# A new written order for all engines of a strided convolution with its gradients

## The chip, the cores and the metric

The kernel runs on one core of a Trainium2 chip. The time is that of one execution on the device, in microseconds (us). A core has several engines with queues of their own: TensorE (PE; its weight loads are listed as PEld), VectorE (DVE), ScalarE (ACT), GpSimd (POOL) and SyncE (SP), which here issues DMA transfers only. Each engine takes its instructions strictly in the order in which they were written; between engines semaphores make an instruction wait for those on whose results it depends.

## What is computed

The forward pass is a convolution over time with stride 2, a normalisation of each channel over all positions, and a tanh-GELU. The kernel returns its output and the gradients by all four inputs for a given output gradient.

```python
B, T, D, K = 2, 16000, 256, 31          # x [2,16000,256], w [31,256,256], bf16

def _fwd_reference(x, w, gn_gamma, gn_beta):
    L = (T - K) // 2 + 1                # 7985
    h = sum of einsum('blc,cd->bld', x[:, i:i + 2 * L:2, :], w[i]) over i < K
    mu = einsum('bld->bd', h)[:, None, :] / L
    var = einsum('bld->bd', (h - mu) ** 2)[:, None, :] / L
    h = (h - mu) / sqrt(var + 1e-5) * gn_gamma + gn_beta
    return gelu(h, approximate=True)

def reference(x, w, gn_gamma, gn_beta, grad_out):
    out, vjp = jax.vjp(_fwd_reference, x, w, gn_gamma, gn_beta)
    return (out, *vjp(grad_out))        # out, dx, dw, dgamma, dbeta
```

## The kernel before

**Stages.** The work is written in five stages, each with its own use of one large SBUF buffer (`arena`; nearly all tiles are pieces of it and bear its name in the profile) and of four PSUM pairs (`ps`).

- F0: convolution of batch 0, in four chunks (`forward`, L709). Three nested levels of a fast algorithm for short filters replace products by sums: DVE forms sums of the input (`tt` of `f_sums`, L509) and of the weights (`w_sub`, L493), PE multiplies (`f_mm`, L551), ACT copies PSUM tiles (`keep`, L646) and DVE adds them as starting values ("seeds", `ve`, L631).
- F1: convolution of batch 1, beside it the statistics and the GELU with its derivative for batch 0 (`gelu_unit`, L901: ACT at L911, L913, L918, L920 and L937, DVE at L916, L922, L926 and L939).
- G0: the input gradient of the first chunks (`input_grad`, L1360; PE at L1235, ACT copies at L1268, seeds at L1312, sums of the results at L1338, sums of planes at L1133), beside it the GELU of batch 1. Four steps prepare the gradient of the convolution's output: `e_load`, `e_comp` (L1096, L1098, L1100 on DVE, L1103 on ACT).
- G1: the rest of the input gradient (`g_planes`, L1183, `g_piece`, L1322). In G0 and G1 `dl_turn` (L1110) transposes what the weight gradient needs: SP issues a transpose (`turn`, L352), POOL stores the result to DRAM (`load`, L347, to tiles `dld`).
- W: the weight gradient in nine rounds n = 0 to 8 (`weight_grad`, L1637). Each round loads gradient tiles (`d_tile`, L1503, from `dld`) and x tiles (`x_raw`, L1468, from DRAM), forms sums (L1466, L1579, L1583, L1594, L1599, L1679, L1684), multiplies (L1513), seeds (`w_both`, L1623) and writes (`w_emit`, L1542). In some rounds `out0_late` (L959) transposes and stores the second batch's output.

**What sets the order.** Helpers such as `add` (L223) do not issue an instruction. `Plan` collects 3469 operations, each with its engine, the function that issues its instructions, and the earlier operations on which it depends (`preds`), worked out from the memory that it reads and writes. The number of an operation is the count of the call of `add` that made it: F0 has 0 to 699, F1 700 to 1250, G0 1251 to 1951, G1 1952 to 2872, W 2873 to 3468. At the end `emit` goes through the constant tuple `SEQUENCE` (L39), which lists every number once, and issues the operations in that order:

```python
assert all(place[p] < place[i] for i, o in enumerate(self.ops) for p in o["preds"])
for i in SEQUENCE:
    r = self.ops[i]["fn"]()
    ...
    pin(r)
```

So an engine's queue is the part of `SEQUENCE` that holds its numbers; DMA issues of SP and POOL are in such queues too. An operation of PE is a group of matmuls, 8 of them in most of G0.

**Operations named below.**

| number | engine, line | what it does |
|---|---|---|
| 259 | SP L347 | writes zeros to a `dld` tile |
| 22 to 29 | SP L347 | loads of weights |
| 1235, 1232 | DVE L631, L509 | last seed of F1, and a sum |
| 1349 | SP L347 | stores a GELU output tile to `yd` |
| 1352, 1354 | ACT L911 | first GELU step of the next tile; overwrites the tile that 1349 reads |
| 1353, 1355 | ACT L913 | second GELU step; DVE 1356 (L916) needs them |
| 1345, 1347 | ACT L937 | copies with a sum; 1346, 1348 (DVE L939) are their partners |
| 1602, 1608 | ACT L646 | keeps of PSUM tiles |
| 1599 | ACT L1268 | copy of a PSUM tile; needs PE 1598 |
| 1603, 1604 | PE L1235 | need 1599 |
| 1609, 1611 | PE L1235 | 1609 needs 1602, 1611 needs 1608; 1608 needs 1603 and 1604 |
| 1606 | PE L1235 | between them |
| 1558, 1620 | DVE L1338, L1133 | sum of a result, sum of planes |
| 1796 | DVE L1061 | scales a plane loaded by 1791 (SP) |
| 1924 | ACT L1268 | copy of a PSUM tile; 1486 and 1897 are ACT too |
| 1951 | DVE L1183 | difference of planes |
| 2839, 2840 | SP L352 | transposes of `dl_turn` |
| 2841, 2842, 2845, 2846 | POOL L347 | stores of their and other results to `dld` |
| 2886, 2885 | SP L347 | `d_tile` loads of round 0 |
| 2944, 2945, 2943 | SP L347 | `x_raw` loads for round 1; 2944 uses memory that the stores read, 2945 waits for PE 2916, 2943 for DVE 2911 |
| 2877 | SP L352 | transpose of `out0_late` |
| 2948, 2949, 2947 | SP L347 | `d_tile` loads of round 1 |
| 2960, 2964 | PE L1513, DVE L1599 | first product and a difference of round 1 |
| 3436 | DVE L631 | seed near the end of W |

Of the kernel before, what the change touches and what calls it, by code (L numbers as in the profile page):

```python
# [34 lines left out]
def mmt(n):  # L35
# [4 lines left out]
    4, 11, 5, 6, 12, 7, 8, 10, 1, 3, 14, 2, 13, 21, 15, 16, 30, 31, 37, 39, 34, 32, 33, 36,  # L40
    40, 35, 19, 38, 41, 42, 46, 43, 49, 17, 45, 51, 44, 48, 52, 53, 50, 18, 54, 55, 47, 60, 20, 66,
    259, 65, 22, 61, 24, 84, 67, 25, 85, 23, 83, 86, 26, 87, 77, 28, 62, 29, 27, 79, 88, 171, 63, 59,
    71, 91, 68, 58, 89, 64, 57, 69, 93, 56, 70, 72, 94, 238, 170, 74, 90, 95, 73, 172, 96, 97, 105, 99,
    98, 101, 75, 107, 106, 111, 100, 92, 112, 102, 108, 76, 109, 113, 110, 130, 123, 122, 131, 114, 104, 196, 124, 137,
    125, 133, 78, 132, 115, 134, 103, 135, 267, 116, 136, 239, 144, 154, 186, 117, 173, 120, 146, 80, 118, 119, 155, 199,
    127, 145, 148, 156, 126, 157, 128, 147, 197, 129, 158, 151, 152, 159, 121, 149, 150, 160, 176, 138, 167, 139, 182, 140,
    177, 198, 174, 141, 142, 168, 161, 162, 153, 143, 201, 163, 169, 166, 207, 202, 183, 203, 175, 206, 178, 251, 200, 187,
    227, 209, 184, 205, 229, 185, 226, 180, 223, 81, 188, 189, 208, 9, 277, 247, 164, 228, 179, 181, 225, 210, 263, 165,
    255, 214, 283, 243, 213, 211, 0, 289, 204, 290, 231, 230, 82, 222, 292, 192, 190, 224, 212, 193, 279, 191, 278, 234,
    215, 312, 280, 232, 291, 313, 281, 216, 282, 235, 293, 381, 218, 220, 299, 194, 217, 219, 300, 236, 301, 302, 237, 297,  # L50
    303, 379, 221, 295, 304, 294, 233, 326, 285, 284, 314, 287, 319, 286, 353, 306, 288, 298, 305, 354, 296, 328, 307, 308,
    195, 327, 352, 309, 315, 378, 329, 310, 316, 317, 330, 318, 311, 337, 333, 336, 356, 332, 334, 340, 355, 331, 341, 349,
    380, 339, 320, 338, 321, 350, 322, 358, 357, 342, 351, 324, 369, 343, 359, 344, 382, 365, 323, 364, 368, 387, 383, 325,
    245, 250, 346, 348, 395, 345, 360, 408, 384, 362, 361, 385, 396, 252, 386, 366, 241, 394, 405, 370, 276, 404, 335, 253,
    264, 397, 242, 420, 371, 388, 271, 406, 367, 249, 390, 240, 246, 426, 363, 389, 258, 392, 432, 257, 409, 268, 254, 455,
    410, 261, 411, 256, 412, 372, 244, 391, 347, 407, 375, 414, 275, 422, 421, 248, 373, 393, 270, 403, 413, 398, 374, 423,
    416, 456, 433, 424, 425, 400, 442, 401, 417, 532, 533, 399, 443, 402, 444, 418, 445, 419, 446, 262, 274, 376, 427, 272,
    269, 447, 457, 497, 428, 462, 531, 448, 435, 434, 430, 265, 260, 449, 377, 495, 429, 450, 436, 529, 441, 431, 458, 439,
    469, 438, 437, 471, 440, 273, 459, 452, 470, 460, 496, 461, 415, 479, 472, 498, 453, 480, 530, 454, 473, 481, 451, 475,
    463, 476, 477, 499, 464, 474, 501, 500, 492, 482, 266, 465, 502, 507, 483, 511, 467, 503, 508, 484, 493, 512, 504, 485,  # L60
    539, 486, 487, 494, 466, 491, 535, 468, 489, 509, 560, 505, 488, 478, 548, 513, 536, 514, 537, 547, 490, 534, 541, 572,
    538, 540, 562, 542, 546, 556, 544, 557, 564, 515, 558, 543, 584, 518, 559, 506, 545, 516, 561, 566, 510, 573, 574, 555,
# [4 lines left out]
    527, 621, 690, 673, 652, 653, 675, 623, 676, 691, 644, 646, 686, 650, 677, 924, 685, 654, 688, 692, 678, 528, 687, 651,  # L67
    945, 679, 699, 680, 938, 645, 693, 931, 695, 925, 664, 667, 946, 711, 944, 681, 930, 932, 683, 689, 694, 655, 969, 657,
    682, 933, 951, 926, 684, 659, 700, 940, 927, 696, 668, 658, 697, 663, 656, 970, 928, 701, 929, 702, 935, 934, 937, 936,
    939, 942, 698, 971, 661, 665, 703, 704, 705, 947, 941, 706, 943, 952, 712, 666, 948, 660, 707, 708, 662, 709, 710, 960,  # L70
    736, 972, 916, 961, 954, 716, 949, 714, 713, 953, 715, 963, 717, 950, 739, 957, 965, 974, 1016, 955, 996, 718, 959, 956,
    962, 737, 973, 975, 720, 976, 977, 721, 719, 731, 958, 964, 984, 967, 732, 966, 983, 722, 986, 979, 723, 724, 733, 734,
    725, 980, 981, 968, 726, 729, 735, 728, 727, 1017, 988, 738, 730, 740, 987, 760, 982, 741, 998, 990, 985, 999, 978, 742,
    989, 997, 1043, 1000, 744, 1001, 743, 745, 1006, 1002, 995, 1007, 746, 991, 1008, 1041, 992, 747, 1004, 763, 748, 761, 749, 1009,
    754, 755, 751, 1003, 1018, 753, 756, 752, 762, 759, 764, 1012, 993, 765, 1010, 750, 766, 1011, 757, 768, 758, 784, 1023, 1005,
    1044, 769, 767, 1019, 1014, 1013, 770, 1024, 771, 785, 994, 1042, 772, 787, 1015, 1025, 773, 1032, 777, 783, 776, 1020, 775, 1033,
    778, 786, 1089, 1021, 1022, 788, 1088, 780, 1029, 1027, 789, 1028, 779, 1026, 1031, 808, 1030, 1068, 790, 1034, 782, 1035, 1039, 781,
    791, 792, 1051, 793, 1037, 794, 804, 809, 1050, 803, 1046, 1053, 795, 774, 796, 1070, 1047, 1036, 1040, 1048, 1038, 1052, 805, 797,
    811, 1069, 807, 799, 800, 1061, 801, 1045, 810, 802, 812, 1059, 832, 1049, 1056, 1054, 806, 813, 1055, 1071, 1114, 1117, 1072, 1073,
    1079, 1058, 1074, 814, 1078, 1113, 816, 1057, 1080, 815, 817, 1060, 1090, 1115, 835, 818, 1067, 819, 833, 1081, 798, 820, 1063, 1075,  # L80
    1116, 821, 824, 823, 1082, 825, 1076, 828, 826, 834, 836, 858, 831, 1062, 1084, 837, 1077, 1158, 838, 1091, 827, 1095, 839, 1083,
    840, 841, 861, 842, 830, 1092, 1093, 829, 1094, 1064, 843, 1066, 1100, 1101, 1086, 1065, 1102, 844, 859, 851, 1103, 1085, 1104, 1096,
    822, 852, 845, 1111, 847, 855, 856, 848, 849, 1130, 850, 860, 1124, 1098, 885, 862, 853, 1087, 1097, 846, 854, 863, 857, 1118,
    864, 1105, 1119, 865, 1112, 866, 1125, 888, 867, 886, 868, 878, 1106, 1099, 869, 1107, 877, 1126, 870, 1132, 1127, 1109, 871, 1131,
    1134, 873, 883, 876, 882, 887, 884, 1129, 1145, 875, 879, 874, 1160, 1128, 889, 1164, 1277, 880, 1108, 1144, 881, 890, 1133, 1147,
    872, 1110, 1146, 1148, 1155, 891, 1263, 1159, 893, 892, 894, 1149, 1150, 904, 895, 896, 905, 897, 1135, 1151, 1170, 1136, 1161, 1162,
    1152, 898, 1137, 1181, 907, 1120, 900, 906, 1138, 908, 901, 1163, 1172, 1154, 902, 899, 903, 1171, 1139, 1180, 1121, 1142, 1275, 1278,
    1279, 1183, 1141, 1280, 1140, 1143, 1174, 1156, 1182, 1267, 909, 1194, 1166, 1290, 1165, 1157, 1173, 1122, 1167, 1177, 1176, 1185, 1193, 1175,
    1168, 1123, 1282, 1184, 1169, 1265, 910, 1187, 1200, 1291, 1178, 1186, 911, 1208, 1196, 1188, 1264, 1195, 1281, 1209, 1190, 1197, 1153, 1210,
    1211, 1198, 1205, 1199, 1179, 1212, 1218, 912, 1191, 1219, 913, 920, 1216, 914, 1202, 1192, 1215, 1201, 917, 1189, 1213, 1221, 1214, 1204,  # L90
    918, 919, 1233, 1203, 1222, 1206, 1269, 1220, 921, 1217, 1223, 1271, 922, 1224, 923, 1234, 1226, 1292, 1237, 1227, 1293, 1230, 1225, 1283,
    1236, 1284, 1268, 1239, 1294, 1238, 1285, 1295, 1321, 1296, 1232, 1286, 1235, 1297, 1298, 1287, 1320, 1266, 1243, 1276, 1288, 1289, 1242, 1207,
    1270, 1309, 1311, 1307, 1330, 1245, 1228, 1308, 1310, 1518, 1312, 1229, 1300, 1240, 1247, 1299, 1520, 1241, 1519, 1244, 1533, 1521, 1522, 1301,
    1526, 1272, 1246, 1322, 1231, 1527, 1323, 1250, 1528, 1303, 1532, 1324, 1304, 1248, 1302, 1545, 1650, 1314, 1273, 1325, 1305, 1306, 1540, 1313,
    1249, 1315, 1539, 1251, 1534, 1316, 1641, 1252, 1538, 1326, 1523, 1253, 1567, 1254, 1317, 1255, 1256, 1535, 1327, 1328, 1524, 1257, 1318, 1544,
    1258, 1649, 1636, 915, 1329, 1274, 1529, 1525, 1259, 1260, 1261, 1262, 1673, 1319, 1334, 1536, 1651, 1541, 1530, 1333, 1640, 1658, 1537, 1562,
    1332, 1549, 1674, 1566, 1542, 1331, 1507, 1652, 1543, 1550, 1563, 1335, 1546, 1531, 1351, 1548, 1570, 1568, 1555, 1653, 1336, 1556, 1571, 1564,
# [1750 lines left out]
```

## Time and profile before

| | us |
|---|---|
| three runs | 1136.36, 1140.59, 1136.03 |
| their median | 1136.36 |
| the profiled execution | 1133.3 |
| its span | 1131.5 |

The span goes from the first to the last instruction of the profiled execution; 1.8 us of that execution's own time lie outside it. The mean granted TensorE clock was 0.995 of full speed.

In the profile a row of the timeline gives the start and the length of a group of like instructions on one engine, the engine, the line, the operation, the tile written and the tile read, the shape, the count, and in square brackets the idle time of the engine ahead of it with the engine and tile that ended this idle time. SPq is the queue of SP: there the length is the time that the queue was taken by the issue. A row of the windows gives, for a stretch, the busy time of each engine with its count, the granted TensorE clock, the busy share of the DMA engines and the rate in GB/s. A row of the waits gives for an engine and line what it waited for: the total, the number of times, the longest.

### The profile page before, as it was taken

The page shows a single profiled execution, that of the slowest core. Times are in us where ns is not written, and L with a number is a line of the kernel's source. Part 1 is how long each engine was busy: PE and PEld are TensorE (multiplying, and loading weights), DVE is VectorE, ACT ScalarE, POOL GpSimd, SP SyncE. Part 2 cuts the span into 40 slices and gives each one's busy share as a digit, 9 for nine tenths or more (in the row PEclk, how much of TensorE's full clock was granted, in tenths as well). Part 3 has the DMA queues.
Part 4 walks back from the last instruction along what each step waited for, and adds up shares of the span by engine and source line. Part 5 has one row for each costly group of instructions (what it writes and reads, how often), then busy time and mean ns, then how long its engine had stood idle before and what let it go on. Part 6 is the DMA issues. An engine that isn't in the chain of part 4 may idle for free. (4 is left out here: it accounts for less than half of the span.)

```text
span 1131.5 us, 19151 instructions
## 1 busy us (share of the span) xinstructions
PE 1097.4 (97%) x7642; PEld 751.2 (66%) x7688; DVE 1029.5 (91%) x1031; ACT 557.3 (49%) x826; POOL 135.9 (12%) x212
## 2 busy tenths in 40 slices
PE   6999999999999989899999999999999999999997
PEld 4888899877777874344444444444488886666786
DVE  7998798769999999899999989889999999889997
ACT  1244444378788669677867666564312212111200
POOL 0000000000000022332222233333110000000000
PEclk9999999999999999899999999999999999999999
DMA  9678868969897799999986687899999707999655
GB/s 233 117 218 207 221 203 231 215 136 204 194 191 211 227 322 288 264 252 266 255 215 183 163 207 204 202 214 220 258 310 230 269 10 256 355 327 299 212 160 159
DMA packets 360407, 251.97 MB, mean 223 GB/s; under 512 B 234487, under 2 KB 327933, under 8 KB 358141
## 3 DMA queue, kind: packets, MB, share of 16 engines
q1 hardware_dynamic: 353213, 231.86, 76.3%
q0 software_dynamic: 7104, 18.89, 6.2%
q8 instruction: 60, 0.98, 0.4%
q14 instruction: 30, 0.25, 0.1%
HBM read 110.43 MB, written 84.45 MB: 172 GB/s over the span
## 5 line engine op out<-in xcount | busy, mean ns | idle before, releaser
L551 PE MATMUL ps<-arena 128*128 128x256 bf16 (+4 forms) x3460 | 407.3, 281 | 12.4 <-DMA arena<-in_x_dram 5.5
L1235 PE MATMUL ps<-arena 128*128 128x512 bf16 x1775 | 390.9, 378 | 9.7 <-ACT ps L1268 4.5
L551 PEld LDWEIGHTS <-arena 128*128 128x128 bf16 x3460 | 337.2, 98 | 82.2 <-issue 6.6
L1235 PEld LDWEIGHTS <-arena 128*128 128x128 bf16 x1812 | 178.1, 98 | 220.8 <-issue 16.8
L1513 PE MATMUL ps<-arena 128*128 128x256 bf16 (+1 forms) x2407 | 300.1, 286 | 5.2 <-DVE ps L1623 1.4
L1513 PEld LDWEIGHTS <-arena 128*128 128x128 bf16 x2416 | 235.9, 98 | 70.1 <-issue 5.4
L646 ACT ACTIVATE arena<-ps 128x1024 f32<-128x1024 f32 x126 | 126.2, 1022 | 255.2 <-PE ps L1513 103.4
L509 DVE TENSOR_TENSOR arena<-arena 128x2080 bf16<-128x2080 bf16 (+7 forms) x125 | 154.8, 1265 | 15.1 <-PE ps L551 14.4
L347 POOL DMA_DIRECT2D dld<-arena x144 | 104.5, 728 | 253.5 <-DMA arena<-arena 228.8
L926 DVE TENSOR_TENSOR arena<-arena 128x2048 bf16<-128x2048 bf16 (+1 forms) x80 | 95.4, 1197 | 3.6 <-ACT arena L918 1.0
L1466 DVE TENSOR_TENSOR arena<-arena 128x4096 bf16<-128x4096 bf16 (+1 forms) x50 | 87.9, 1775 | 7.1 <-DMA arena<-in_x_dram 6.2
L1312 DVE TENSOR_TENSOR ps<-ps,arena 128x1024 f32<-128x1024 f32 x60 | 72.5, 1227 | 6.6 <-PE ps L1235 3.5
L1183 DVE TENSOR_TENSOR arena<-arena 128x1032 bf16<-128x1032 bf16 (+1 forms) x110 | 72.4, 691 | 4.5 <-PE ps L1235 2.4
L666 ACT ACTIVATE arena<-ps 128x512 bf16<-128x512 f32 (+1 forms) x64 | 37.0, 580 | 53.2 <-PE ps L551 49.3
L356 POOL MEMSET arena<- 128x128 bf16 (+9 forms) x31 | 8.2, 286 | 400.5 <-DVE arena L509 239.4
L1615 ACT COPY ps<-ps 128x256 f32<-128x256 f32 x54 | 19.2, 359 | 70.5 <-PE ps L1513 69.3
L1322 DVE TENSOR_TENSOR arena<-ps,arena 128x1024 bf16<-128x1024 f32 x40 | 48.3, 1219 | 4.4 <-PE ps L1235 4.2
L1599 DVE TENSOR_TENSOR arena<-arena 128x2048 bf16<-128x2048 bf16 x42 | 50.5, 1221 | 0.0
L916 DVE SCALAR_TENSOR_TENSOR arena<-arena 128x2048 bf16<-128x2048 bf16 (+1 forms) x16 | 35.8, 2239 | 14.1 <-ACT arena L913 7.4
L587 ACT ACTIVATE ps<-ps 128x256 f32<-128x256 f32 x72 | 26.7, 370 | 39.8 <-PE ps L551 38.7
L1583 DVE TENSOR_TENSOR arena<-arena 128x2048 bf16<-128x2048 bf16 x38 | 45.5, 1220 | 0.1
L911 ACT ACTIVATE arena<-arena,stats 128x1024 bf16<-128x1024 bf16 (+1 forms) x32 | 37.9, 1212 | 8.8 <-DMA yd<-arena 8.8
(89 smaller groups left out, 794.9 us busy)
## 6 DMA issues: line engine op xcount, KB each, us to landing
arena<-in_x_dram SPq DMA_DIRECT2D x24, 1024.0 KB
dld<-arena POOLq DMA_DIRECT2D x144, 128.0 KB, 4.0
arena<-in_x_dram SPq DMA_DIRECT2D x34, 512.0 KB
out_dram<-arena SPq DMA_DIRECT2D x31, 512.0 KB
arena<-hd SPq DMA_DIRECT2D x24, 512.0 KB
arena<-dld SPq DMA_DIRECT2D x18, 640.0 KB
arena<-dld SPq DMA_DIRECT2D x18, 576.0 KB
vl<-arena SPq DMA_DIRECT2D x36, 256.0 KB
```

Of the source, the lines that this page charges most:

```text
L347: lambda: e.dma_start(out=out, in_=in_), dma=np_ * ns / 16e3 * 1.03, ns=ns, tp=SH[pk], slack=slack)
L509: lambda: nc.vector.tensor_tensor(out=o, in0=a, in1=b, op=ALU.add))
L551: yield nc.tensor.matmul(ps[:, dh, cs], lhsT=wt, rhs=mv, start=s0, stop=False, skip_group_check=True)
L646: lambda: nc.scalar.activation(out=out, in_=ps, func=ACT.Copy, scale=scale))
L926: add("DVE", dve(nf), [o], [a, b_], lambda: V.tensor_tensor(out=o, in0=a, in1=b_, op=op))
L1183: lambda: nc.vector.tensor_tensor(out=o, in0=a, in1=b, op=ALU.subtract))
L1235: yield nc.tensor.matmul(ps[:, e, 0:wide], lhsT=lt, rhs=mv, start=s0, stop=False, skip_group_check=True)
L1312: lambda ps=ps, g=g: nc.vector.tensor_tensor(out=ps[:], in0=px[:], in1=g, op=ALU.add))
L1322: lambda: nc.vector.tensor_tensor(out=ho[:, :, k, :], in0=ps[:], in1=g, op=ALU.add))
L1466: add("DVE", dve(o.free_size()), [o], [a, b], lambda: nc.vector.tensor_tensor(out=o, in0=a, in1=b, op=ALU.add))
L1513: yield nc.tensor.matmul(ps[:, s, c0:c1], lhsT=lt, rhs=mv, start=s0, stop=False, skip_group_check=True)
L1599: add("DVE", dve(2048), [o], [u, v], lambda o=o, u=u, v=v: nc.vector.tensor_tensor(out=o, in0=u, in1=v, op=ALU.subtract))
```

## The change

Only the tuple `SEQUENCE` is different. It holds the same 3469 numbers, so the same instructions on the same tiles are issued, and every operation still comes behind those on which it depends. The change describes itself as planned anew on twelve draws of varying transfer times and means of two profiles.

Instructions whose place in the queue of their engine is another one: 169 of 931 on PE (by up to 5 places), 280 of 999 on DVE (up to 11), 152 of 689 on ACT (up to 12), 95 of 208 on POOL (up to 7), 282 of 642 on SP (up to 9). They lie in many short blocks over the whole kernel, within which the numbers are rearranged; between the blocks the queues agree.

All 136 lines that are replaced are lists of such numbers. Below are those that hold the operations of the table.

```diff
@@ -37,151 +37,151 @@
-    259, 65, 22, 61, 24, 84, 67, 25, 85, 23, 83, 86, 26, 87, 77, 28, 62, 29, 27, 79, 88, 171, 63, 59,
...
-    1654, 1578, 1646, 1341, 1575, 1647, 1600, 1655, 1553, 1648, 1352, 1781, 1579, 1557, 1342, 1354, 1343, 1576, 1602, 1598, 1577, 1346, 1605, 1344,
-    1345, 1780, 1583, 1558, 1599, 1347, 1603, 1620, 1350, 1609, 1353, 1348, 1604, 1355, 1796, 1606, 1608, 1356, 1610, 1611, 1560, 1582, 1623, 1357,
...
-    1236, 1284, 1268, 1239, 1294, 1238, 1285, 1295, 1321, 1296, 1232, 1286, 1235, 1297, 1298, 1287, 1320, 1266, 1243, 1276, 1288, 1289, 1242, 1207,
...
-    1923, 1926, 1897, 1904, 1489, 1982, 1924, 1909, 1951, 1941, 2042, 1912, 1952, 1487, 1930, 1908, 1981, 1933, 1490, 1986, 1491, 2044, 1928, 1985,
...
-    2856, 2834, 2850, 2888, 2862, 2857, 2886, 2851, 2858, 2839, 2863, 2893, 2885, 2883, 2859, 2866, 2864, 2861, 2894, 2946, 2841, 2865, 2907, 2845,
-    2899, 2846, 2908, 2895, 2842, 2900, 2903, 2901, 2868, 2904, 2896, 2902, 2897, 2869, 2906, 2898, 2905, 2913, 2912, 2867, 2915, 2944, 2870, 2860,
-    2950, 2914, 2891, 2872, 2871, 2892, 2916, 2911, 2910, 2919, 2945, 2923, 2943, 2917, 2909, 2924, 2920, 2928, 2936, 2947, 2948, 2930, 2935, 2877,
-    2929, 2931, 2937, 2921, 2940, 2980, 2918, 2932, 2922, 2952, 2933, 2938, 2951, 2949, 2941, 2880, 2939, 2954, 2934, 2925, 2953, 2942, 2966, 2960,
...
-    3435, 3440, 3451, 3379, 3436, 3386, 3390, 3437, 3447, 3397, 3456, 3452, 3448, 3444, 3458, 3453, 3445, 3402, 3449, 3457, 3398, 3446, 3400, 3459,
...
+    24, 65, 22, 61, 84, 83, 25, 85, 23, 67, 86, 28, 87, 77, 259, 29, 62, 26, 27, 79, 88, 59, 63, 89,
...
+    1292, 1225, 1284, 1238, 1294, 1268, 1239, 1240, 1285, 1321, 1295, 1296, 1232, 1297, 1286, 1235, 1298, 1287, 1320, 1270, 1243, 1276, 1308, 1288,
...
+    1340, 1646, 1781, 1578, 1654, 1341, 1601, 1647, 1655, 1579, 1553, 1648, 1352, 1342, 1598, 1602, 1557, 1576, 1343, 1354, 1577, 1620, 1599, 1344,
+    1605, 1345, 1796, 1780, 1558, 1583, 1347, 1348, 1609, 1582, 1353, 1604, 1346, 1603, 1560, 1355, 1350, 1606, 1608, 1356, 1610, 1611, 1623, 1357,
...
+    1475, 2009, 1913, 1478, 1484, 1906, 1910, 1482, 1903, 1896, 1483, 1883, 1914, 1882, 1485, 1899, 1878, 1923, 1900, 1895, 1925, 1924, 1950, 1486,
...
+    1945, 1951, 2002, 1943, 1953, 1998, 1952, 1946, 2001, 1944, 1996, 1947, 1995, 1500, 1911, 2004, 1997, 2003, 1501, 2012, 2000, 1502, 2013, 2037,
...
+    2839, 2855, 2834, 2850, 2829, 2886, 2888, 2862, 2857, 2885, 2851, 2858, 2946, 2863, 2842, 2859, 2846, 2866, 2841, 2907, 2894, 2845, 2893, 2908,
+    2865, 2864, 2895, 2904, 2899, 2903, 2896, 2868, 2906, 2944, 2900, 2897, 2912, 2901, 2869, 2902, 2898, 2913, 2867, 2905, 2915, 2870, 2891, 2872,
+    2914, 2950, 2871, 2892, 2860, 2916, 2861, 2911, 2923, 2910, 2919, 2945, 2943, 2924, 2917, 2909, 2936, 2877, 2935, 2928, 2920, 2930, 2980, 2929,
+    2931, 2937, 2922, 2940, 2921, 2918, 2932, 2948, 2949, 2952, 2947, 2880, 2933, 2951, 2938, 2954, 2941, 2939, 2953, 2934, 2925, 2966, 2942, 2960,
...
+    3420, 3428, 3422, 3424, 3430, 3396, 3377, 3429, 3427, 3403, 3431, 3438, 3425, 3432, 3439, 3426, 3433, 3434, 3442, 3391, 3436, 3443, 3435, 3397,
```

249 rows, old and new, of the table SEQUENCE are left out of this document.

## The prediction

> **What bounds the kernel now.** I read the page's head first, then the waits of PE, then the windows by stage, then the timeline around the longest stalls.
>
> ```profile
> span 1131.5 us, 19151 instructions
> PE 1097.4 (97%) x7642; PEld 751.2 (66%) x7688; DVE 1029.5 (91%) x1031; ACT 557.3 (49%) x826; POOL 135.9 (12%) x212
> ...
> PE ps L551 <- DMA arena<-in_x_dram: 5.5, 2, 4.5
> PE ps L1235 <- ACT ps L1268: 4.5, 2, 3.5
> PE ps L551 <- DVE ps L631: 3.5, 1, 3.5
> ```
>
> TensorE is busy 1097.4 of 1131.5 us, so 34.1 us are all that an order can win: instructions and durations stay, only idle time can go. The waits (total, times, longest) show that one third of it is three places. The first, 5.5, is the first x load; nothing is written ahead of it that could move. The others are one stall of 3.5 at L1268 and one of 3.5 at L631.
>
> ```profile
> 380.00:416.00 36.00, 32.71 (x326) 31.66 (x325) 35.93 (x47) 20.30 (x44) 0.74 (x5) 1.00 0.81 290
> 467.00:588.00 121.00, 120.37 (x560) 55.84 (x571) 113.47 (x130) 90.94 (x97) 38.47 (x60) 1.00 1.00 253
> 588.00:606.00 18.00, 16.03 (x72) 7.04 (x72) 17.93 (x23) 10.77 (x15) 4.58 (x8) 1.00 0.53 150
> 610.00:790.00 180.00, 176.88 (x809) 80.68 (x824) 162.41 (x212) 114.15 (x124) 56.10 (x86) 1.00 0.82 205
> 826.40:847.20 20.80, 19.57 (x179) 17.24 (x177) 20.80 (x18) 1.94 (x2) 0.00 (x0) 1.00 0.93 307
> 849.00:909.00 60.00, 58.20 (x526) 51.03 (x524) 60.00 (x42) 15.59 (x24) 0.00 (x0) 1.00 0.79 235
> 912.00:1041.00 129.00, 128.63 (x924) 90.72 (x930) 119.25 (x84) 24.31 (x40) 0.00 (x0) 1.00 0.78 255
> 1042.00:1121.00 79.00, 78.26 (x653) 63.84 (x653) 78.60 (x60) 8.30 (x16) 0.53 (x1) 1.00 0.60 186
> ```
>
> The columns are the window, its length, busy time of PE, PEld, DVE, ACT and POOL, the granted clock, DMA share and rate. Two kinds of stage alternate. In 467 to 588, 610 to 790 and 912 to 1041 PE is the bound. In 380 to 416, 588 to 606, 826 to 909 and 1042 to 1121 DVE has no idle time: a PE stall there is DVE work that PE waits for, and no exchange of neighbours removes it unless DVE comes there earlier or does something else first. So the change can win at a few places only.
>
> **Part 1: the stall at 416 (F1 into G0), 0.**
>
> ```profile
> 410.00:420.00 10.00, 6.48 (x57) 5.37 (x56) 10.00 (x11) 8.18 (x22) 3.25 (x2) 1.00 0.99 350
> ...
> 414.90 1.22 DVE L631 TENSOR_TENSOR ps<-ps,arena 128x1024 f32<-128x1024 f32 x1
> 416.18 1.06 PE L551 MATMUL ps<-arena 128*128 128x231 bf16 x9 [3.46 <-DVE ps L631]
> ```
>
> PE waits 3.46 us for DVE's seed 1235. DVE is busy all 10 us around it, and the new order leaves the same operations ahead of 1235 (the six of `e_comp`, 1232): only their order among each other differs. The stall stays: 0.
>
> **Part 2: the stall at 460 (G0), -2.5.**
>
> ```profile
> 444.74 11.85 PE L1235 MATMUL ps<-arena 128*128 128x512 bf16 x53
> 455.22 2.37 ACT L911 ACTIVATE arena<-arena,stats 128x1024 bf16<-128x1024 bf16 x2 [3.03 <-DMA yd<-arena]
> 457.50 1.00 ACT L646 ACTIVATE arena<-ps 128x1024 f32<-128x1024 f32 x1
> 459.44 0.58 ACT L1268 COPY ps<-ps 128x512 f32<-128x512 f32 x1
> 460.07 8.10 PE L1235 MATMUL ps<-arena 128*128 128x512 bf16 x24 [3.47 <-ACT ps L1268]
> 463.40 2.29 DVE L916 SCALAR_TENSOR_TENSOR arena<-arena 128x2048 bf16<-128x2048 bf16 x1 [3.73 <-ACT arena L913]
> 465.38 1.01 ACT L646 ACTIVATE ps<-ps 128x1024 f32<-128x1024 f32 x1 [2.02 <-PE ps L1235]
> ...
> 460.00:470.00 10.00, 9.88 (x34) 4.10 (x35) 5.92 (x7) 7.95 (x9) 1.56 (x3) 0.72 1.06 331
> ```
>
> ACT stands 3.03 us in L911 (1352) until store 1349 has read the buffer that it overwrites; then come 1354, the keep 1602, 1345 and only then the copy 1599, on which PE 1603 waits 3.47 us. The next 24 matmuls take 8.10 us, 0.338 each, against 11.85/53 = 0.224 before: another 24 x 0.114 = 2.7 us, with a granted clock of 0.72 in that window.
>
> The new ACT order is 1352, 1602, 1354, 1599, 1345; that of PE puts 1609, which needs only 1602, ahead of 1604 and 1603. Store 1349 is where it was, so 1352 still starts at 455.22. At ACT's pitch (1.14 an L911, 1.0 a keep) 1602 ends at 457.4 and 1599 at 459.0. PE is free at 456.60 (460.07 - 3.47), so it stands 0.9 us instead of 3.47; its 24 matmuls run at 0.216 to 0.224 and end near 462.7 instead of 465.38. What is late next is ACT: 1608, the keep behind these matmuls, is queued behind the same set as before (to 1355, which ends at 463.4, where DVE's L916 begins), so it starts at 463.4 instead of 465.38, and PE is earlier by 2.0 through 1608, and by up to 2.8 at 1611, which before also waited behind the slow 1606 and a weight load. DVE moves 1796 (0.5 us, waits for load 1791) ahead of 1558, 1348 and 1346; its cover is the 3.73 us for which DVE stands idle ahead of 463.40 and which stays, as 1355 ends no earlier.
>
> ```profile
> DVE arena L1338 <- PE ps L1235: 1.9, 3, 0.9
> ...
> DVE arena L1133 <- PE ps L1235: 0.6, 1, 0.6
> ```
>
> How much of 2.8 lasts? From 467 to 588 PE has no stall to absorb it, but at 588 DVE is the bound, so PE's lead counts there only as far as DVE leads too. Between 420 and 600 DVE waited 1.9 + 0.6 = 2.5 us for PE; that is what it can gain. I take -2.5, bounds 0 (DVE uses its idle time otherwise) and -2.8.
>
> [...]
>
> **Part 3: the end of G0 (588 to 606), -0.7.**
>
> ```profile
> 589.68 8.85 PE L1235 MATMUL ps<-arena 128*128 128x512 bf16 x39 [1.05 <-ACT ps L1268]
> 589.77 0.69 DVE L1183 TENSOR_TENSOR arena<-arena 128x1032 bf16<-128x1032 bf16 x1
> ```
>
> PE stands 18.00 - 16.03 = 2.0 us here. ACT's copy 1924 goes ahead of 1486 and 1897; DVE's 1951 (0.69) goes behind eleven others, so the DVE operations that PE waits for come 0.69 earlier, and 1951 itself falls into 610 to 790, where DVE has 17.6 us of idle time. -0.7, bounds 0 and -2.0.
>
> **Part 4: G1 (610 to 790), 0.** PE stands 180.00 - 176.88 = 3.1 us in many stalls under 1 us. The moves here are exchanges of neighbours; half put what PE waits for earlier, half later. 0, bounds -3.1 and +3.
>
> **Part 5: start of W (804 to 860), -1.5.**
>
> ```profile
> 817.08 1.20 SPq L352 DMA_TRANSPOSE arena<-arena  x1
> 821.89 2.98 POOL L347 DMA_DIRECT2D dld<-arena  x4 [9.04 <-DMA arena<-arena]
> 825.12 1.36 DVE L1679 TENSOR_TENSOR arena<-arena 128x2304 bf16<-128x2304 bf16 x1 [1.23 <-DMA arena<-dld]
> 833.28 4.51 SPq L347 DMA_DIRECT2D arena<-in_x_dram  x2
> 841.72 11.32 SPq L352 DMA_TRANSPOSE arena<-yd  x1
> 848.53 2.29 DVE L1466 TENSOR_TENSOR arena<-arena 128x4096 bf16<-128x4096 bf16 x1 [1.30 <-DMA arena<-in_x_dram]
> 853.08 0.58 SPq L347 DMA_DIRECT2D arena<-dld  x1
> 853.15 9.02 PE L1513 MATMUL ps<-arena 128*128 128x256 bf16 x81 [0.93 <-DVE arena L1583]
> 859.69 2.55 DVE L1684 TENSOR_TENSOR arena<-arena 128x4608 bf16<-128x4608 bf16 x1
> ```
>
> DVE, the bound from here to 909, stands twice: 1.23 us for d_tile load 2885 and 1.30 us for x load 2943. In SP's queue the transpose 2839 (817.08) stood behind 2886, a load that waits for stores; now 2840 and 2839 come first, so POOL's four stores (821.89) and x load 2944 behind them start some 3 us earlier, and SP reaches 2945 and 2943 without a queue; these then wait for PE 2916 (its end, 831.5, is not moved) and so start at most 1.8 us earlier than 833.28. Both gaps together are 2.53. 2885 is again behind 2886, so its gap goes only in part. -1.5, bounds 0 and -2.5. From 909 to 1041 PE has no stall, so a gain lasts.
>
> **Part 6: the rest, -1.1.**
>
> ```profile
> 10.14 0.82 SPq L347 DMA_DIRECT2D dld<-zt  x1
> 19.56 5.41 PE L551 MATMUL ps<-arena 128*128 128x512 bf16 x36 [0.80 <-DVE arena L493]
> 1108.41 5.40 PE L1513 MATMUL ps<-arena 128*128 128x256 bf16 x48 [0.40 <-DVE ps L1623]
> ```
>
> SP's 259 (0.82) moves behind five weight loads, which so start 0.8 us earlier; PE's 0.80 behind them shrinks by half, and with smaller stalls of F0 I take -0.7 (bounds 0, -1.3). Near the end 3436, on which PE waits, moves three places forward: -0.4 (0, -0.7). The stores after the last matmul stay.
>
> **Sum:** 0 - 2.5 - 0.7 + 0 - 1.5 - 1.1 = -5.8 us. The profiled execution, 1133.3 us (span 1131.5 and 1.8 around it), becomes 1127.5. The runs' median, 1136.36, lies 3.1 above it; the same step gives 1130.6.
>
> **Rivals.** (a) *DVE gives it back*: PE's lead of part 2 is lost at 588 or at 826, where DVE has no idle time at all; only the head, part of W and the end stay, about -2: 1134.4. For it: the two windows with DVE at 17.93 of 18.00 and 60.00 of 60.00. Against: the 2.5 us in which DVE waited for PE.
>
> (b) *G1's small stalls go too*: another 3.1 to 4 less, 1127. For it: nothing but their number; against: the moves go both ways.
>
> (c) *Slower, one mechanism: loads behind the long transpose.* 2877, which kept SP 11.32 us from 841.72, now stands ahead of the three d_tile loads 2948, 2949 and 2947 of the second round of W; before, only 2949 was behind it. PE's 2960 (853.15) and DVE's 2964 wait for such loads. If 2877 starts at 834 to 838, they are issued at 845 to 849. The one that was behind it before took at most 6.0 us from 853.66 to its use at 859.69, so they land between 851 and 855 by that row. It decides from 851.6 on, the time at which PE would reach 2960 with part 5's gain; at 857, with the DMA engines full, PE and DVE lose 5.4, and part 5 is gone as well: -5.8 + 1.5 + 5.4 = +1.1, and with the phase of part 1 against us (+2.7) +3.8. Price: 1137.5 to 1140.2.
>
> [...]
>
> **How the numbers follow.** Forecast .42, (a) .34, (b) .11, (c) .13. The range goes from 1124 (the forecast with the outer bounds of parts 4, 3, 5, 2 and 6: 3.1 + 1.3 + 1.0 + 0.3 + 0.9 = 6.6 less) to 1139 (the middle of (c)). 0.5% is 5.7 us, about what a measurement can tell here, so faster means below 1130.7: half of the forecast's cases with most of those of (b) and luck in the clock, .42; same takes (a), the rest of the forecast and part of (c), .43; slower .15.
>
> **What would show it.** Right: PE's idle ahead of the matmuls at 456 to 460 is about 0.9 and the granted clock of 460 to 470 is 1.00; DVE's gaps at 825 and 848 are under 1 us together; the stall at 416 is again near 3.5. Wrong: a new PE stall over 2 us near 855 behind arena<-dld (c); the end of G0 at the same time as before in spite of a clean 460 (a); a store 1349 that lands later, by which ACT starts later than 455.2 and the whole of part 2 shrinks, since that time is taken as given.

## The result and the profile after

The changed kernel takes 1127.53 us (median of 5 runs, 1124.6 to 1129.43), the kernel before 1136.03 in the runs beside them: ratio 0.9919, 95% interval 0.9893 to 0.9945, so 6.2 to 12.2 us less. In a second set it took 1128.0 us (6 runs) against 1135.74: 0.9944, interval 0.9928 to 0.9960. The forecast was 1130.6 with a range of 1124 to 1139. The sign is as forecast and the size within the range; of the reasons, some are not.

The profiled execution after took 1129.43 us, the slowest of its five. That of before (1133.3) was faster than every one of the five runs of before. The two traces therefore differ by less than the kernels do, 3.8 us in span. The page's head and the first waits of PE after the change:

```profile
span 1127.7 us, 19164 instructions
...
PE 1095.8 (97%) x7642; PEld 752.1 (67%) x7688; DVE 1029.9 (91%) x1031; ACT 557.7 (49%) x826; POOL 134.1 (12%) x212
```

```profile
PE ps L551 <- DMA arena<-in_x_dram: 6.2, 2, 4.5
PE ps L1235 <- DVE ps L1312: 5.0, 4, 1.8
PE ps L551 <- DVE ps L631: 3.4, 1, 3.4
```

The stall on ACT's L1268 (4.5 before) is no longer among them, that on the seed of L631 is as it was, and waits on L1312 have grown from 1.0 to 5.0. The windows of after:

```profile
410.00:420.00 10.00, 6.57 (x55) 5.77 (x53) 10.00 (x11) 7.76 (x21) 3.01 (x2) 0.87 0.91 335
...
460.00:470.00 10.00, 9.56 (x47) 4.49 (x46) 8.57 (x13) 8.98 (x11) 1.83 (x4) 1.00 1.18 270
...
588.00:606.00 18.00, 15.55 (x71) 6.84 (x71) 17.84 (x23) 10.30 (x13) 4.48 (x8) 1.00 0.49 138
```

The clock near 416 is now the reduced one (0.87) and that of 460 to 470 is full. ACT and PE around 460, in the timeline:

```profile
455.62 1.24 ACT L911 ACTIVATE arena<-arena,stats 128x1024 bf16<-128x1024 bf16 x1 [0.72 <-DMA yd<-arena]
456.77 1.00 ACT L646 ACTIVATE arena<-ps 128x1024 f32<-128x1024 f32 x1
...
458.81 0.58 ACT L1268 COPY ps<-ps 128x512 f32<-128x512 f32 x1
```

```profile
455.55 8.79 PE L1235 MATMUL ps<-arena 128*128 128x512 bf16 x40 [0.74 <-DVE arena L1338]
464.73 3.62 PE L1235 MATMUL ps<-arena 128*128 128x256 bf16 x16 [0.39 <-ACT ps L646]
```

PE stands 0.74 and 0.39 us instead of 3.47, without the slow matmuls after it. ACT's own wait for store 1349 is shorter too, 0.72 us instead of 3.03, which the prediction had taken as unchanged. At the start of W (SP, DVE and PE):

```profile
790.01 13.39 SPq L352 DMA_TRANSPOSE arena<-arena  x3
803.46 0.58 SPq L347 DMA_DIRECT2D arena<-in_x_dram  x1
...
838.19 11.20 SPq L352 DMA_TRANSPOSE arena<-yd  x1
849.45 1.52 SPq L347 DMA_DIRECT2D arena<-dld  x3
```

```profile
810.58 2.29 DVE L1466 TENSOR_TENSOR arena<-arena 128x4096 bf16<-128x4096 bf16 x1 [2.19 <-DMA arena<-in_x_dram]
...
853.61 8.57 PE L1513 MATMUL ps<-arena 128*128 128x256 bf16 x77 [0.91 <-DMA arena<-dld]
```

Here is a new stall of DVE, 2.19 us for x load 2873 (issued at 803.46), and a small one of PE behind transpose 2877. Last, the end. In both pairs the first row is SP's last issues, the second DVE's last operations; before, then after:

```profile
1123.36 5.24 SPq L347 DMA_DIRECT2D out_dram<-arena  x6
...
1124.75 0.42 DVE L1542 TENSOR_TENSOR arena<-ps,arena 128x256 bf16<-128x256 f32 x1 [0.19 <-PE ps L1513]
```

```profile
1123.81 1.38 SPq L347 DMA_DIRECT2D out_dram<-arena  x3
...
1123.58 0.76 DVE L1542 TENSOR_TENSOR arena<-ps,arena 128x256 bf16<-128x256 f32 x2 [0.52 <-PE ps L1513]
```

Before, the last data were ready at 1125.17 but SP issued the last store until 1128.60; after, 1124.34 and 1125.19.

### The profile page after: what moved, and what is told of

It reads as the page before. It is cut to its first block, busy times and chain, and to the rows that moved or that the text cites. A ratio compares the mean times of both kernels' runs of the same rounds, so it can differ in the third digit from the quotient of the medians.

```text
span 1127.7 us, 19164 instructions
## 1 busy us (share of the span) xinstructions
PE 1095.8 (97%) x7642; PEld 752.1 (67%) x7688; DVE 1029.9 (91%) x1031; ACT 557.7 (49%) x826; POOL 134.1 (12%) x212
## 5 line engine op out<-in xcount | busy, mean ns | idle before, releaser
L551 PE MATMUL ps<-arena 128*128 128x256 bf16 (+4 forms) x3460 | 409.7, 282 | 12.2 <-DMA arena<-in_x_dram 6.2
L1466 DVE TENSOR_TENSOR arena<-arena 128x4096 bf16<-128x4096 bf16 (+1 forms) x50 | 87.8, 1778 | 5.2 <-DMA arena<-in_x_dram 5.0
L1312 DVE TENSOR_TENSOR ps<-ps,arena 128x1024 f32<-128x1024 f32 x60 | 72.6, 1228 | 7.2 <-PE ps L1235 3.6
L916 DVE SCALAR_TENSOR_TENSOR arena<-arena 128x2048 bf16<-128x2048 bf16 (+1 forms) x16 | 35.8, 2237 | 9.5 <-ACT arena L911 6.1
L621 ACT ACTIVATE arena<-ps 128x512 f32<-128x512 f32 x56 | 29.6, 602 | 26.7 <-DVE ps L631 15.4
```

Of the source, the lines that this page charges most:

```text
L551: yield nc.tensor.matmul(ps[:, dh, cs], lhsT=wt, rhs=mv, start=s0, stop=False, skip_group_check=True)
L1312: lambda ps=ps, g=g: nc.vector.tensor_tensor(out=ps[:], in0=px[:], in1=g, op=ALU.add))
L1466: add("DVE", dve(o.free_size()), [o], [a, b], lambda: nc.vector.tensor_tensor(out=o, in0=a, in1=b, op=ALU.add))
```

## The experiments

One trace each of 14 orders shows how far single executions differ. The table gives, from each trace, the time from the end of one PE operation to the end of another, the same two in all orders (the heads are their ends in the trace of before); the last column is from the last such operation, at 1123.0, to the end of the span. The labels are those of the runs below.

| order | 407 to 440 | 440 to 470 | 407 to 608 | 608 to 789 | 789 to 905 | end |
|---|---|---|---|---|---|---|
| before | 33.40 | 29.58 | 201.24 | 181.52 | 116.00 | 8.54 |
| p_tail | 33.40 | 27.63 | 203.52 | 180.50 | 114.77 | 5.71 |
| tail_min | 34.85 | 30.77 | 204.43 | 180.86 | 116.78 | 5.91 |
| p_w | 34.84 | 28.32 | 204.20 | 181.65 | 113.73 | 8.77 |
| p_g1 | 34.84 | 27.71 | 203.75 | 179.17 | 117.01 | 8.54 |
| p_early | 34.74 | 30.11 | 203.77 | 180.54 | 115.02 | 8.53 |
| b_min | 34.83 | 26.47 | 202.16 | 179.52 | 115.65 | 8.51 |
| g0_rest | 34.84 | 25.89 | 200.68 | 179.38 | 117.12 | 8.61 |
| p_g0 | 35.91 | 24.53 | 200.59 | 179.86 | 117.35 | 8.52 |
| after | 34.74 | 25.07 | 200.82 | 179.33 | 117.21 | 5.91 |
| after_again | 35.98 | 25.35 | 200.74 | 179.13 | 117.48 | 5.92 |
| turn_last | 35.95 | 24.53 | 198.29 | 179.17 | 117.61 | 5.86 |
| seed_first | 35.22 | 24.53 | 197.15 | 179.41 | 117.17 | 5.96 |
| x_early | 35.71 | 24.53 | 197.68 | 179.47 | 114.41 | 5.87 |

From 407 to 608 the six traces with the old order of G0 (before to p_early in the table) take 203.5 us on average, and the trace of before, the one that the prediction read, is the shortest of the six.

**Parts of the change, one at a time.** Each order is that of before with the new order only among the operations of one stretch of the tuple.

```diff
-SEQUENCE = before
+SEQUENCE = before[:p] + [i for i in after if i in before[p:q]] + before[q:]
 # p_early 0:1289, p_g0 1289:1953, p_g1 1953:2763, p_w 2763:3385, p_tail 3385:3469
```

**p_tail.** 

> Order of before, with the new order only among the operations that were written last (from about 1085 us on). Theory A (the prediction: what follows the last matmul stays, only seed 3436 comes earlier): 0.4 us less. Theory B (the two traces: SP's queue holds out0_late stores until the end, so that the last store is issued 3.0 us behind its data before and at once after): 2.6 to 3.0 us less, all of it between the last matmul and the end of the span; the last matmul ends within 0.3 us of before's place against the DVE work ahead of it.

It took 1132.46 us, ratio 0.9958 (0.9941 to 0.9975). The end takes 5.71 instead of 8.5 us. Theory B holds: the end of the kernel changed, where the prediction had left it alone. The times show more (2.8 to 6.7 us less) than the 2.8 us of the trace.

**tail_min**, SP's queue alone:

```diff
-3397, 3445, 3402, 3398, 3446, 3400, 3401
+3397, 3402, 3400, 3398, 3445, 3446, 3401
```

> Order of before; on SP's queue alone three out0_late stores (3402, 3398, 3400) go directly behind 3397, ahead of the w_emit store 3445, which waits for DVE. Nothing else is moved. Theory B (the queue of SP sets the end): as p_tail, 2 to 3 us less. Theory A (the end is set by the last products and their stores): no change.

1134.42 us, ratio 0.9973 (0.9953 to 0.9993). SP's last issues and DVE's last operation of this order:

```profile
1123.79 5.60 SPq L347 DMA_DIRECT2D out_dram<-arena  x6
...
1127.78 0.42 DVE L1542 TENSOR_TENSOR arena<-ps,arena 128x256 bf16<-128x256 f32 x1 [0.19 <-PE ps L1513]
```

The last store now leaves SP at 1129.39, 1.2 us behind its data at 1128.20, where before it was 3.4. The cause is the place of three stores. In the order of before they were queued behind a store that waits for DVE, and SP had to issue them all at the end; here they go out ahead of it.

**p_g0.** 

> Order of before, new order only among the operations from about 420 to 606 us (G0). Theory A (the prediction): the stall of 3.47 at 460 shrinks to 0.9 with a clock of 1.00, of which 2.5 last, and 0.7 at the end of G0: 3.2 us less. Theory B (DVE gives it back): PE is 2.8 or more ahead at 467, but at 606 no more than 1 us ahead: 0 to 1 us less.

1130.58 us, ratio 0.9946 (0.9928 to 0.9965), the largest part. From 407 to 608 the trace takes 200.59 us against 203.5 on average, but only 0.65 less than the trace of before; 440 to 470 takes 24.53.

**p_w.** 

> Order of before, new order only among the operations from about 790 to 1085 us (start and middle of W). Theory A (the prediction): both DVE gaps (1.23 and 1.30) go, 1.5 us less. Theory B (the two traces): x load 2873 lands late and DVE waits 2.19 for it in place of them, PE behind it: 0 to 1 us more. Theory C (transpose 2877 ahead of the d_tile loads): a stall of 2 us or more at PE 2960 near 853 and 1 to 4 us more.

1134.61 us, ratio 0.9984 (0.9966 to 1.0001). 789 to 905 takes 113.73 us where the eight traces with the old order there take 114.8 to 117.4, 116.2 on average (two of the eight, p_g0 and p_g1, have the clock at half there for 3.4 us). Theory A, as far as the interval goes; neither B nor C shows.

**after_again**, the changed kernel itself. 

> The changed kernel itself, once more, so that it and its parts are compared with the same runs of before. Theory A (the parts add up: tail 0.9958, G0 0.9946, W 0.9984 and G1 near 1): ratio near 0.989. Theory B (the parts stand in each other's way, as G1's new order puts x load 2873 late for W's): ratio 0.991 to 0.994.

0.9944 (0.9928 to 0.9960). The five parts multiply to 0.990 (0.9958 x 0.9946 x 0.9984 x 1.0001 x 1.0010); the two measurements of the whole are 0.992 and 0.994. Each interval is about 0.002 to either side, so the times alone don't decide between A and B. The table speaks for B: 789 to 905 takes 117.2 to 117.6 us in the changed order, 113.73 where only that part is new.

**p_g1.** 

> Order of before, new order only among the operations from about 606 to 790 us (G1). Theory A (the prediction: exchanges of neighbours, nothing lasts): within 1 us of before. Theory B (from the stage times of the traces, 179.3 us in the changed kernel against 179.9 to 181.7 in five traces with the old order): 1 to 2 us less in G1, part of it given back at the start of W if x load 2873 is issued after 803 and DVE waits for it.

1135.15 us, ratio 1.0001 (0.9983 to 1.0019). In the trace G1 takes 179.17 us, just below the 179.4 to 181.7 with the old order, and the next stage 117.01, near its high end. Nothing lasts.

**p_early.** 

> Order of before, new order only among the operations up to about 420 us (F0 and F1). Theory A (the prediction): 0.7 us less, as the weights land 0.8 earlier. Theory B (the first x load sets the start, and its landing varies by itself): no change within 1 us.

1136.38 us, ratio 1.0010 (0.9993 to 1.0027). Theory B by the median: no gain from the earlier weight loads shows, though the 0.7 us of theory A lie just inside the interval.

**b_min**, the part of the stall at 460 alone, on ACT and then PE:

```diff
-1352, 1354, 1602, 1345, 1599, 1347
+1352, 1602, 1354, 1599, 1345, 1347
-1605, 1603, 1609, 1604, 1606
+1605, 1609, 1604, 1603, 1606
```

> Order of before; on ACT only the keep 1602 goes ahead of 1354 and the copy 1599 ahead of 1345, and on PE 1609 goes ahead of 1603 and 1604, as in the new order. Nothing else is moved. Theory A (ACT's order alone makes the stall at 460): the stage from 440 to 470 us takes about 25 us instead of 28 to 31 and the whole 3 to 6 us less, as with the whole of G0. Theory B (DVE's and SP's moves in G0 carry it): under 2 us less.

1135.43 us, ratio 1.0005 (0.9986 to 1.0024): no gain. Its PE rows show that the stall did shrink. Later rows, of DVE, PE and the windows, show a place where part of the lead went:

```profile
459.01 1.02 PE L1235 MATMUL ps<-arena 128*128 128x512 bf16 x4 [0.62 <-ACT arena L646]
460.62 3.61 PE L1235 MATMUL ps<-arena 128*128 128x512 bf16 x16 [0.59 <-ACT ps L1268]
465.91 4.26 PE L1235 MATMUL ps<-arena 128*128 128x256 bf16 x19 [1.68 <-ACT ps L646]
```

```profile
579.47 2.36 DVE L497 TENSOR_TENSOR arena<-arena 128x2048 bf16<-128x2048 bf16 x2 [2.66 <-DMA dld<-arena]
...
590.01 11.34 PE L1235 MATMUL ps<-arena 128*128 128x512 bf16 x43 [2.61 <-ACT ps L1268]
...
590.75:594.10 3.35, 3.35 (x10) 1.18 (x9) 3.09 (x4) 1.79 (x2) 0.68 (x2) 0.50 0.47 95
```

440 to 470 takes 26.47 us, 2.6 less than the 29.0 of the old order on average. 407 to 608 takes 202.16, only 1.3 less than the average, so half of it is lost again behind 470. Counted from the operation at 440, as in the table, PE is 3.0 us ahead of the six's average at 587 and 1.4 at 593. Operation 1913 (DVE L497) had stood 2.66 us at 579, as it overwrites memory that POOL's stores have yet to read; PE then stands 2.61 us at 590 (2.1 on average of the six), and after that the clock is at half for 3.4 us, which is so in p_tail and p_g1 at this place too. So most of what is lost here goes with the clock, and only about 0.4 us with the longer stall. The 1.3 us that are left don't show in the times, but lie within their interval (from 1.6 us less to 2.7 more).

**g0_rest**, the counterpart: p_g0 with these queues put back.

```diff
-1352, 1602, 1354, 1599, 1345, 1347
+1352, 1354, 1602, 1345, 1599, 1347
-1605, 1609, 1604, 1603, 1606
+1605, 1603, 1609, 1604, 1606
```

> The new order in G0 alone, as before in this study, but with ACT's 1602, 1354, 1345, 1599 and PE's 1603, 1604, 1609 in the order of before: all of G0's change without the part that was tried alone. Theory A (the stall at 460 carries G0's gain, though alone it showed none): the stall ahead of 1603 is 3 us or more again and the ratio to before is near 1. Theory B (the other moves of G0 carry it): ratio near 0.995 in spite of that stall, as DVE, which is full at 588 to 606, reaches its work there earlier. Between the two (0.997 to 0.998): both parts are needed.

1131.99 us, ratio 0.9953 (0.9933 to 0.9973): theory B, nearly all of p_g0's gain without the exchange that b_min tried. What was not expected is that the stall at 460 is small here too. ACT and PE there:

```profile
455.85 2.37 ACT L911 ACTIVATE arena<-arena,stats 128x1024 bf16<-128x1024 bf16 x2 [0.69 <-DMA yd<-arena]
...
456.03 4.48 PE L1235 MATMUL ps<-arena 128*128 128x512 bf16 x20 [0.98 <-DVE arena L1338]
```

ACT waits 0.69 us for store 1349, where it waited 2.5 to 3.3 in the six traces with the old order. So other moves in G0 shorten this stall as well; which of them was not tried. The rows that follow are from the end of G0, first of g0_rest, then of p_w, which has the old order in G0:

```profile
579.75 2.35 DVE L497 TENSOR_TENSOR arena<-arena 128x2048 bf16<-128x2048 bf16 x2
...
589.86 10.50 PE L1235 MATMUL ps<-arena 128*128 128x512 bf16 x45 [0.57 <-ACT ps L646]
```

```profile
582.28 2.36 DVE L497 TENSOR_TENSOR arena<-arena 128x2048 bf16<-128x2048 bf16 x2 [2.63 <-DMA dld<-arena]
...
589.63 1.75 ACT L918 ACTIVATE arena<-arena 128x1856 bf16<-128x1856 bf16 x1 [5.39 <-DVE arena L916]
...
592.19 0.59 ACT L1268 COPY ps<-ps 128x512 f32<-128x512 f32 x1
592.83 7.34 PE L1235 MATMUL ps<-arena 128*128 128x512 bf16 x33 [3.29 <-ACT ps L1268]
```

With the old order 1913 waits for POOL's stores in all seven traces (0.50 us in that of before, 1.5 to 2.7 in the other six), and PE stands 1.1 to 3.3 us behind ACT's L1268 some 10 us later. With the new order it waits in one trace of seven only (that of after, 2.47 us, there for a transpose), and PE's stall on L1268 is gone in those seven. On DVE 1922 and 2009 now stand ahead of 1913; whether this or the earlier stores do it was not tried by themselves.

By the rows, what takes PE's stall away is another move. The copy at L1268 is 1924. In the old order ACT's queue has it behind 1486 (L918), which waits for DVE's L916, and this stands behind 1913. In the new order 1924 goes ahead of 1486, as the trace of after shows, where 1913 does wait:

```profile
585.13 0.57 ACT L1268 COPY ps<-ps 128x512 f32<-128x512 f32 x1 [1.59 <-PE ps L1235]
...
586.65 1.75 ACT L918 ACTIVATE arena<-arena 128x1856 bf16<-128x1856 bf16 x1 [0.95 <-DVE arena L916]
```

So the place of 1924 decides whether PE stands behind L1268, and 1913's wait helps to set how long. No order moves 1924 alone, so this is read from the rows and not tried.

**x_early**, the changed kernel with one exchange on SP:

```diff
-2784, 2783, 2836, 2873, 2835
+2784, 2783, 2873, 2836, 2835
```

> The changed kernel with one more exchange: on SP's queue x load 2873 goes ahead of transpose 2836, which in the changed kernel stood from 796.65 to 800.85 for two stores while 2873's own memory was free from 787.6. Theory A (the changed order loses at the start of W what it could win, because 2873 is behind that wait): 2873 is issued near 797 instead of 803.5, DVE's wait of 2.19 ahead of 2887 goes, the stage from 790 to 835 takes 45.5 instead of 48.3 us, and the whole 1.5 to 2.5 us less than the changed kernel (ratio to before near 0.991). Theory B (DVE is held up there by PE or the stores as well): the stage stays near 48.

1126.59 us (1123.61 to 1127.63), ratio 0.9918 (0.9904 to 0.9933). SP and DVE:

```profile
786.90 6.81 SPq L352 DMA_TRANSPOSE arena<-arena  x2
793.76 0.58 SPq L347 DMA_DIRECT2D arena<-in_x_dram  x1
...
805.19 2.28 DVE L1466 TENSOR_TENSOR arena<-arena 128x4096 bf16<-128x4096 bf16 x1
```

The load leaves 9.7 us earlier than in the trace of after (3.1 of them because this trace is ahead at 789 already), DVE waits for nothing at L1466, and 789 to 905 takes 114.41 us instead of 117.2 to 117.6. Theory A, as to the place and the size in the trace. The whole has the lowest median of all orders tried, about 1 us below the changed kernel's, but the intervals of the two ratios overlap. The place of 2836 is not the whole cause. p_w has the same two neighbours as the changed kernel, but there SP does not wait for the stores, and the three transposes ahead of 2873 take 8.39 us, where they take 11.3 to 13.4 in the four traces of the changed order without this exchange:

```profile
795.14 8.39 SPq L352 DMA_TRANSPOSE arena<-arena  x3
803.58 0.58 SPq L347 DMA_DIRECT2D arena<-in_x_dram  x1
```

**seed_first**, the changed kernel with the seed of the stall at 416 earlier on DVE:

```diff
-1284, 1294, 1285, 1232, 1235
+1284, 1232, 1235, 1294, 1285
```

> The changed kernel with DVE's 1232 and 1235 ahead of two sums of e_comp (1294 and 1285) at 412. Theory A (the stall at 416 is DVE work ahead of the seed that could stand behind it): PE waits about 1.2 us instead of 3.45 for 1235, the granted clock does not fall after it, and of the 2.2 us about 1 lasts, as ACT's copies behind 1294 and 1285 are now later for PE 1300. [...]

1127.81 us, ratio 0.9930 (0.9912 to 0.9949). PE and, by windows, its clock:

```profile
414.47 2.54 PE L551 MATMUL ps<-arena 128*128 128x231 bf16 x24 [1.17 <-DVE ps L631]
419.93 0.58 PE L1235 MATMUL ps<-arena 128*128 128x512 bf16 x1 [2.92 <-POOL arena L1084]
```

```profile
417.00:420.00 3.00, 0.08 (x2) 0.10 (x2) 2.02 (x3) 3.00 (x8) 0.96 (x3) 0.87 0.66 228
420.00:422.00 2.00, 1.78 (x4) 0.59 (x6) 2.00 (x3) 1.59 (x8) 0.09 (x1) 0.50 0.82 277
```

The stall only splits: 1.17 and then 2.92 behind POOL's copies, and the stage takes 35.22 us. Theory A holds for the wait for 1235 alone, not for the sum and not for the clock: it falls to 0.50, and does so within the stall of 2.92 us (0.87 on average from 417 to 420).

**turn_last**, the changed kernel with the d_tile loads ahead of the long transpose:

```diff
-2943, 2877, 2948, 2949, 2947
+2943, 2948, 2949, 2947, 2877
```

> The changed kernel with the d_tile loads 2948, 2949 and 2947 ahead of the transpose 2877, as two of the three were in the order of before. Theory A (the rival of the prediction: 2877 holds these loads up): they are issued near 838 to 840 instead of 849.5 to 851, PE's wait of 0.91 at 2960 and DVE's of 0.47 at 2969 for arena<-dld go, 0.5 to 1 us less in the stage from 835 to 905. Theory B (their landing is covered by DVE's work): that stage stays within 0.3 us of 69.0.

1127.43 us, ratio 0.9924 (0.9904 to 0.9943). SP, PE and DVE:

```profile
836.87 3.53 SPq L347 DMA_DIRECT2D arena<-dld  x3
```

```profile
851.45 8.80 PE L1513 MATMUL ps<-arena 128*128 128x256 bf16 x79 [0.30 <-DVE arena L1583]
```

```profile
846.83 2.29 DVE L1466 TENSOR_TENSOR arena<-arena 128x4096 bf16<-128x4096 bf16 x1 [1.40 <-DMA arena<-in_x_dram]
```

The waits for arena<-dld are gone, but DVE now stands 1.40 us for x load 2943, whose transfer has three more beside it (that these hold it up is not shown by itself); 789 to 905 takes 117.61 us. Theory B in the sum: as much is lost as is won.

## Why the prediction was right, and where it was not

- **Part 1** (the stall at 416 stays): right. It is 3.43 to 3.46 us in every order but seed_first, where its successor takes its place. The stage took 33.40 us in two traces and 34.7 to 36.0 in the other twelve: the reduced clock at this stall is the usual case, and the trace of before is one of the two without it. No run shows the "phase of part 1" of rival (c), nor its 2.7 us at this place. What the runs showed is a price of 1.3 to 1.5 us where the clock is low for 3.4 us (after) and 2.3 to 2.6 where it is for 6.8 (p_g0, after_again, turn_last, x_early).
- **Part 2** (-2.5): the place came out as forecast (waits under 1 us, full clock), the credit did not. The step that failed is "how much of 2.8 lasts": b_min, which has this exchange alone, measured 1.0005, so at most 1.6 us less. Its trace does bear out that nothing absorbs the lead up to 588 (3.0 us at 587). At 590 it falls to 1.4, behind DVE's wait for POOL's stores and with the clock at half. The prediction had looked only at DVE's waits for PE. Rival (a), a lead given back, is thus shown in part, and why the times show no gain at all stays open. Also, store 1349 was taken as unmoved; with the new order in all of G0 ACT waits for it 1.0 us at most, and g0_rest has a short stall at 460 without the exchange on ACT.
- **Part 3** (-0.7): mis-sized. PE's stall before L1268 was 1.05 us in the trace read and is 1.6 to 3.3 in six other traces with the old order; the new order removes it. The cause was named, ACT's 1924 ahead of 1486 and 1897, but the price was taken from DVE's 1951 (0.69 us), and that the stall behind 1924 grows with 1913's wait for the stores was not seen. G0 as a whole: 0.9946, or 6.1 us, against 3.2 forecast for parts 2 and 3.
- **Part 4** (0): right, 1.0001.
- **Part 5** (-1.5): right for the stretch alone (0.9984, 1.8 us). In the whole kernel it is lost: SP's wait in 2836 for POOL's stores (4.1 us in the trace of after), which p_w does not have, stands ahead of 2873. That move was not weighed, though the prediction went through the queue from 2839 on; which other moves make the stores late there stays open. Rival (c) exists as a wait of 0.91 us, not 5.4: the loads were issued at 849.5 to 851, just behind the 845 to 849 that were forecast, and landed in time for most of the work.
- **Part 6** (-1.1): no gain shows at the head (1.0010; 0.7 less lies just inside the interval), and the 0.4 for 3436 was not tried by itself. "The stores after the last matmul stay" is the plain error: that end is 2.6 to 2.8 us shorter in all traces with the new end, and this alone is worth 0.9973 in tail_min. The prediction had checked the last stores' places, not what was queued ahead of them.

The sum of 5.8 us against the 6.4 to 9.2 that the ratios give (0.0056 and 0.0081 of 1136) came out near by luck: the gain at G0's end, which was priced too low, and that of the last stores, which was missed, made up for a credit that showed no gain by itself and for the loss at the start of W.

What stays open: p_tail and p_g0 gain more in their times than their own traces show (4.8 against 2.8, and 6.1 against 2.9 by the stage's average). For p_g0, 1.6 us of this is the low clock at 416, which lasts longer in its trace than in the others: from 440 to 608 alone it is 4.5 us below the six's average. But the six traces with the whole new order of G0 differ among themselves by 4 us there (161.9 to 166.1), so one trace an order is too few to say where the rest lies.

## What to carry to other kernels

A trace is one execution: DVE's wait in 1913 for POOL's stores went from 0.50 to 2.7 us over the seven traces with the old order, PE's stall on L1268 behind it from 1.1 to 3.3, and the trace that was read had the smallest of both. Before crediting a shorter stall, follow the engine that is full afterwards through all its waits, those on DMAs too. At the end of a kernel read the queue that issues the last stores: what stands in it behind a waiting store is issued after it, however long ready. Here the last store left 3.4 us behind its data, and 1.2 with three stores moved ahead of the waiting one.

## What the runs showed of the hardware

In these traces the clock's fall isn't bound to one length of the stall. In the trace of before PE stands idle from 456.60 to 460.07, and the clock is at half before this stall is over:

```profile
456.60:458.80 2.20, 0.00 (x0) 0.00 (x0) 2.20 (x3) 2.20 (x3) 1.30 (x2) 1.00 0.97 355
458.90:460.00 1.10, 0.00 (x0) 0.00 (x0) 0.77 (x3) 1.10 (x4) 0.05 (x1) 0.50 1.86 53
```

PE's rows and windows of p_g1, and then of p_w:

```profile
461.64 8.54 PE L1235 MATMUL ps<-arena 128*128 128x512 bf16 x31 [2.77 <-ACT ps L1268]
...
462.00:467.00 5.00, 5.00 (x18) 1.90 (x16) 2.04 (x1) 3.82 (x5) 0.00 (x0) 0.66 1.15 283
```

```profile
463.18 7.07 PE L1235 MATMUL ps<-arena 128*128 128x512 bf16 x32 [3.98 <-ACT ps L1268]
...
462.00:467.00 5.00, 3.82 (x18) 1.75 (x18) 1.90 (x4) 5.00 (x8) 0.72 (x2) 1.00 1.10 330
```

After 2.77 us the granted clock fell (0.66 on average, 18 matmuls in 5 us), after 3.98 us it stayed full; in seed_first it fell within a stall of 2.92. In the trace of before it fell 2.2 to 2.3 us after the last matmul ahead of the stall. Like stalls end differently: at 460 tail_min and p_early, with stalls of 4.1 and 3.9 us, have 0.50 from 462 to 467, where p_w has 1.00; at 416 the clock is 1.00 in the trace of before, behind a stall of 3.46 us, and 0.87 in that of after, behind 3.4. In the clock records of the 14 traces, from 20 us to the last matmul, the granted clock is at half in 23 stretches, 16 of them 3.4 us long (that of after from 417.3) and 7 of them 6.8 (that of before from 458.9). What decides whether a stall ends with the low clock is not shown.
